# A fused attention, Fourier and feed-forward kernel: ScalarE and GpSimd in program order, weight splits two products ahead

## The chip, the core and the metric

The kernel runs on one core of a Trainium2 chip. The metric is the device time of one execution in microseconds (us), as the median of several runs. The core has five engines that run side by side: TensorE (PE in the profile, with its weight loads as PEld), VectorE (DVE), ScalarE (ACT), GpSimd (POOL) and SyncE (SP), which here issues the DMA transfers. Each engine works through its own list of instructions in the order in which the program was compiled; semaphores make one engine wait for another.

## What is computed

For each of 8 batches (8 heads, 576 tokens, head width 64): 32 packed queries attend to all keys, and all 576 queries attend to the 32 packed results. The result `x` is Fourier-transformed over tokens and over features, and a feed-forward network follows:

```
p_packed = softmax(p k^T / 8) v
x        = softmax(q p_packed^T / 8) p_packed        # 576 x 512 after joining heads
u        = x + real(fft(fft(x, tokens), features))
un       = (u - mean(u)) / sqrt(var(u) + 1e-6)
out      = u + relu(un @ w_ch1) @ w_ch2              # 512 -> 2048 -> 512
```

Products that need more than the fast matmul format's precision are done as three matmuls of split operands: `x = hi + lo`, ScalarE rounds `hi` (`wr_h`, `uh`, `fh`, ...), and VectorE or GpSimd subtracts to get `lo` (`wr_l`, `ul`, `fl`, ...).

## The kernel before

The 36 blocks of 128 token rows (four per batch, and one for each pair of batches with the rows left over, `R`) form nine tiles of four blocks, numbered 0 to 8 here. The loop at L698 runs the feed-forward network of one tile (`ffn`, L605) and, spread between its products, the attention and Fourier work of the next batch (`front`, L227).

A tile has 16 hidden slices. `up(j)` (L613) is 12 matmuls into the single bank `ph`; ScalarE then takes the relu into `hh` (L629) and VectorE makes `hl` (L630), which frees `ph`. `down(j)` (L633) is 12 matmuls into the four `acc` banks. TensorE's order is up(0), up(1), down(0), up(2), down(1), ..., up(15), down(14), down(15). Between the products stand 32 places, `step(0)` to `step(31)`: step 2j follows up(j), and step 2j+1 follows down(j-1). Each step draws one piece from the generator `front`, up to its next `yield`. The pieces of batches 2 to 7 stand in the third string of `ORDER` (L44), where `y` is a yield: `S` scores, `t` turned scores, `p` packed values, `d` their parts, `g` values spectrum, `U` queries, `e` less one, `m` less mean, `a` weights, `f` `r` `h` folded and their parts, each with a head group 0 or 1. After them come the two Fourier stages (`py`, L486, in steps 23 and 24) and twice spectrum and values (`pz`, `px`, steps 25 to 28). What is left of a batch, the rows `R`, is drawn first in the next tile (`chain`, L700): its spectra in step 0, its values in step 1, directly ahead of `S`.

Before the change the third string puts `S` in step 1, `t0 t1` in step 4, `p0 p1` in 5, `d0 d1` in 6, `g0` in 7, `g1` in 8, `U` in 9, `e0` in 10, `e1` in 11, and `m0 a0 m1 a1 f0 r0 h0 f1 r1 h1` in 12 to 21.

The order of work on an engine is set in two ways. From tile 1 on (L713) the engines in `MANUAL` (L52: PE and DVE) keep program order; ScalarE, GpSimd and SyncE are ordered at compile time by a planner, which goes by its own estimate of times. In tile 0 and ahead of it the planner orders all engines.

Weights: `wsplit` (L599) splits one 128x512 slice into `wr_h` (ScalarE) and `wr_l` (GpSimd), six buffers, so three slices. `up(j)` splits `w1[j]` just ahead of its own matmuls, and `w2[j]` behind the relu. At the end of a tile the next tile's blocks lose their mean (`less`, L579, tile `un`), are transposed between the matmuls of up(15), down(14) and down(15) (`moves`, L584, tile `untp`), and are split (`parts`, L593). `statistics` (L205) sums squares on ScalarE (`junk`), and `deviations` (L199) finishes the rows that are waiting at the next yield.

PSUM banks are given out in turn by `bank` (L93): three shared ones, `ph`, and the four `acc`. The loads of keys, values and queries share two buffers (`ld`).

Of the kernel before, what the change touches and what calls it, by code (L numbers as in the profile page):

```python
# [17 lines left out]
P = 128  # L18
S = 576
# [24 lines left out]
         "S y y y t0 t1 y p0 p1 y d0 d1 y g0 y g1 y U y e0 y e1 y m0 y a0 y m1 y a1 y f0 y r0 y h0 y f1 y "  # L44
         "r1 y h1 y y")
# [6 lines left out]
MANUAL = {mybir.EngineType.PE, mybir.EngineType.DVE}  # L52
# [26 lines left out]
def tile_kernel(ctx, tc, kpT, qT, v, w1, w2, tabC, tabS, tabR, tabB, tabT, sel, ident_d, out):  # L79
# [117 lines left out]
    late = []  # L197

    def deviations():  # L199
        while late:  # L200
            st = stat_of[late.pop(0)]
            nc.vector.tensor_scalar(st[:, 2:3], st[:, 2:3], 1.0 / DM, 1e-6, ALU.mult, ALU.add)  # L202
            nc.gpsimd.tensor_tensor(st[:, 2:3], st[:, 2:3], mhalf, ALU.pow)

    def statistics(key):  # L205
        st = stat_of[key]
        nc.vector.tensor_scalar(st[:, 1:2], st[:, 0:1], 1.0 / DM, None, ALU.mult)  # L207
        junk = work.tile([P, DM], F32, tag="tmp", name="junk", bufs=3)
        nc.scalar.activation(junk, u_of[key], AF.Square, bias=st[:, 1:2], scale=-1.0, accum_out=st[:, 2:3])  # L209
        late.append(key)  # L210
# [16 lines left out]
    def front(b):  # L227
# [3 lines left out]
        eos, fs, sums, turned = {}, {}, {}, {}  # L231
# [52 lines left out]
        def turned_scores(g):  # L284
            e1, sm2 = e1s[g], sums[g]
            ri = small.tile([P, 1], F32, tag="ri", name="ri")
            nc.vector.tensor_scalar(ri, sm2[:, 0:1], sm2[:, 1:2], 1e-9, ALU.add, ALU.add)
            nc.vector.reciprocal(ri, ri)
            rinv[g] = ri
            et = work.tile([P, 5, P], F32, tag="att", name="e1T", bufs=ATT)  # L290
            tp = bank("e1tp")
            for c in range(4):
                nc.tensor.transpose(tp[:, c * P:(c + 1) * P], e1[:, c * P:(c + 1) * P], ident)
            nc.scalar.copy(et[:, 0:4, :].rearrange("p c k -> p (c k)"), tp)
            if b < 2 or g == 0:
                turned["tq"] = bank("e1tq")
            tp = turned["tq"][:, g * P:(g + 1) * P]
            nc.tensor.transpose(tp[:D], e1[:, 4 * P:S], ident)
            nc.vector.tensor_copy(et[:D, 4, :], tp[:D])
            e1T[g] = et  # L300

        def packed(g):

            if g not in vts:
                load_values(g)
            vt = vts[g]
            po = bank("po")
            for c in range(5):
                kk = P if c < 4 else D
                for h in range(4):  # L310
                    nc.tensor.matmul(  # L311
                        po[h * NPK:(h + 1) * NPK, :D], e1T[g][:kk, c, h * NPK:(h + 1) * NPK],
                        vt[:kk, c, h * D:(h + 1) * D], start=(c == 0), stop=(c == 4),
                        tile_position=(0, h * NPK))
            pp2 = work.tile([P, 2, D], F32, tag="pp2", name="pp2")
            nc.vector.tensor_scalar(pp2, po[:, :D].unsqueeze(1).to_broadcast([P, 2, D]), rinv[g], None, ALU.mult)
            pp2s[g] = pp2

        def packed_parts(g):
# [12 lines left out]
            bd = work.tile([P, 4, D], F32, tag="tmp", name="bd", bufs=3)  # L332
            nc.gpsimd.tensor_tensor(bd, pp2[:, 0:1, :].to_broadcast([P, 4, D]),
                                    bmask.unsqueeze(2).to_broadcast([P, 4, D]), ALU.mult)
            hi = work.tile([P, 4 * D], F32R, tag="bdh", name="bdh")
            lo = work.tile([P, 4 * D], F32R, tag="bdl", name="bdl")
            split(hi, lo, bd.rearrange("p a d -> p (a d)"), nc.gpsimd)
            bdh[g], bdl[g] = hi, lo
# [19 lines left out]
        def less_one(g):  # L358

            s2 = s2s[g]  # L360
            m = small.tile([P, 18], F32, tag="m18", name="m18")
            nc.vector.tensor_reduce(m, s2, AX.X, ALU.max)  # L362
            engs[g].tensor_tensor(s2, s2, broadcast(m), ALU.subtract)  # L363
            nc.scalar.activation(s2, s2, AF.Exp, scale=0.125)
            nc.scalar.activation(s2, s2, AF.Copy, bias=-1.0)
# [12 lines left out]
        def values_spectrum(g):  # L378
# [19 lines left out]
            split(hi, lo, prod[0], TW[TL[min(b, 2)]])  # L398
            gh[g], gl[g] = hi, lo

# [22 lines left out]
        def folded_rest(g):  # L423
# [22 lines left out]
            sm.tensor_scalar(f[:, FA + 33:FA + 64], a[:, NE + 256:S], 2.0, 1.0 / 16, ALU.mult, ALU.add)  # L446

        def folded_parts(g):

            eo, f = eos[g], fs[g]  # L450
            ec, oc = eo[:, 0, :], eo[:, 1, :]
            hi = work.tile([P, FW], F32R, tag="fh", name="fh")
            lo = work.tile([P, FW], F32R, tag="fl", name="fl")
            split(hi, lo, f)
            fh[g], fl[g] = hi, lo
            hi = work.tile([P, 256], F32R, tag="xh", name="xh")
            lo = work.tile([P, 256], F32R, tag="xl", name="xl")
            nc.scalar.activation(hi, ec[:, 0:256], AF.Copy, bias=1.0 / 16)
            nc.vector.scalar_tensor_tensor(lo, ec[:, 0:256], 1.0 / 16, hi.bitcast(F32), ALU.add, ALU.subtract)
            xh[g], xl[g] = hi, lo  # L460
            hi = work.tile([P, 256], F32R, tag="oh", name="oh")
            lo = work.tile([P, 256], F32R, tag="ol", name="ol")
            split(hi, lo, oc[:, 0:256], (nc.vector, nc.gpsimd)[EO[min(b, 2)]])
            oh[g], ol[g] = hi, lo

        parts = {"S": lambda _: scores(0, 1), "U": lambda _: queries(0, 1), "s": scores, "t": turned_scores, "p": packed, "d": packed_parts, "q": queries, "e": less_one,
                 "m": less_mean, "g": values_spectrum, "a": weights, "f": folded, "r": folded_rest,
# [4 lines left out]
        for x in ORDER[min(b, 2)].split():  # L472
            if x == "y":
                yield
                deviations()
            else:
                parts[x[0]](int(x[1:] or 0))
# [57 lines left out]
        for c in range(2):  # L535
# [16 lines left out]
            deviations()  # L552
# [46 lines left out]
    def wsplit(src):  # L599
        hi = work.tile([P, DM], F32R, tag="wr", name="wr_h", bufs=6)  # L600
        lo = work.tile([P, DM], F32R, tag="wr", name="wr_l", bufs=6)
        split(hi, lo, src, nc.gpsimd)
        return hi, lo

    def ffn(first, turned, step, nxt, alone):  # L605
# [7 lines left out]
        def up(j, moves=()):  # L613
            moves = list(moves)
            wh, wl = wsplit(w1f[:, j, :])
# [5 lines left out]
            for t in (slice(i, i + step) for i in range(0, T, step)):  # L621
                for k in range(12):
                    c, (l, r) = k // 3, ((wh, uh), (wh, ul), (wl, uh))[k % 3]
                    nc.tensor.matmul(ph[:, t], l[:, c * P:(c + 1) * P], r[:, c, t], start=(k == 0), stop=(k == 11))  # L624
                    if moves:
                        moves.pop(0)()
            hh = work.tile([P, 512], F32R, tag="hh", name="hh")
# [3 lines left out]
            return (hh, hl) + wsplit(w2f[:, j, :])  # L631

        def down(j, hh, hl, vh, vl, moves=()):  # L633

            moves = list(moves)
            for i in range(n):
# [5 lines left out]

        prev = None
        for j in range(NJ):
            last = nxt is not None and j == NJ - 1
            cur = up(j, nxt.moves(0) + nxt.moves(1) if last else ())
# [6 lines left out]
            if nxt is not None and j == NJ - 2:  # L655
                nxt.less(0)
                nxt.less(1)
            if prev is not None:
                down(j - 1, *prev, [lambda: None] * 8 + nxt.moves(2) if last else ())
            step(2 * j + 1)  # L660
            if last:
                nxt.parts(2)
# [4 lines left out]
        deviations()  # L667
# [25 lines left out]
    deviations()  # L693
    spare.clear()
    rest = iter(())
    for j in range(ORDER[0].count("D"), LEAD):
        load_weights(j)
    for t, (first, tk) in enumerate(tiles):  # L698
# [118 lines left out]
```

## Time and profile before

| | us |
|---|---|
| median of 3 runs (lowest, highest) | 1069.37 (1067.02, 1071.57) |
| the profiled execution's own time | 1067.58 |
| its span, first to last instruction | 1065.8 |
| ahead of the first feed-forward product | 59.3 |
| tile 0, to the last output of it | to 200.8 |
| tiles 1 to 6, one batch's front in each | 200.8 to 884.2, 113.2 to 115.0 each |
| tile 7, with the rest of batch 7 alone | 91.9 |
| tile 8, with no front | 85.7 |

A tile's end is taken here where VectorE begins the last of the four instructions of L670 (`u` plus the network's result). Matmuls are pipelined: a 128x512 matmul is shown as 0.39 us long, and the next one starts 0.23 us behind it. So an idle time that the profile shows for PE leaves out what the modelled end covers.

### The profile page before, as it was taken

What the parts mean: (1) busy time and instruction counts of PE and PEld (TensorE: products, weight loads), DVE (VectorE), ACT (ScalarE), POOL (GpSimd) and SP (SyncE); (2) the same over time, 40 slices, a digit from 0 to 9 for tenths busy, and PEclk for the clock granted to TensorE, in tenths of its full rate; (3) what the DMA queues carried; (4) which work ended last, traced back from release to release, by engine and by line L of the source; (5) the groups of instructions that cost most, each with busy time, mean ns of one, the idle gap of its engine ahead of it and who ended that gap; (6) DMA issues with size and microseconds to landing.
All of it is one profiled execution on the core that took longest, in us unless ns stands there. A gap on an engine that the chain in (4) does not pass through costs nothing.

```text
span 1065.8 us, 15006 instructions
## 1 busy us (share of the span) xinstructions
PE 992.6 (93%) x5692; PEld 793.2 (74%) x5692; DVE 598.0 (56%) x1296; ACT 435.4 (41%) x883; POOL 471.2 (44%) x419
## 2 busy tenths in 40 slices
PE   6488888999999999999999999899999999999998
PEld 2366667767877788778877787678777888888886
DVE  4889999547553764468444846475537743113112
ACT  3544454434343444344443444344434443333332
POOL 1545644354444543455335433544445434444442
PEclk8689999999999999999999999999999999999999
DMA  8216433210012100310022002110030001001001
GB/s 328 96 45 209 131 111 101 89 65 28 2 40 95 47 2 1 115 66 1 1 90 92 1 1 83 52 47 1 31 104 1 1 2 40 1 1 40 1 1 40
DMA packets 17743, 58.65 MB, mean 55 GB/s; under 512 B 2081, under 2 KB 2465, under 8 KB 17670
## 3 DMA queue, kind: packets, MB, share of 16 engines
q1 hardware_dynamic: 17670, 57.68, 15.9%
q8 instruction: 45, 0.74, 0.3%
q14 instruction: 28, 0.23, 0.1%
HBM read 48.24 MB, written 9.44 MB: 54 GB/s over the span
## 4 chain that ended last, share of the span: by engine, by line
PE 70%; DVE 16%; ACT 7%; POOL 3%; issue 3%; DMA 1%; SPq 0%; ACTq 0%; DVEq 0%; POOLq 0%
PE ph L624 32%; PE acc L639 26%; ACT wr_h L100 2%; ACT hh L629 2%; PE untp L589 2%; POOL wr_l L101 2%; DVE turned L397 1%; DVE hl L630 1%; DVE s L363 1%; PE po L311 1%; DVE ubuf L547 1%; DVE m L362 1%; DVE turned L393 1%; PE s L255 1%; DVE w2f L181 1%
## 5 line engine op out<-in xcount | busy, mean ns | idle before, releaser
L101 POOL TENSOR_TENSOR wr_l<-w1f,wr_h 128x512 fp32r<-128x512 f32 x144 | 192.2, 1334 | 303.2 <-ACT wr_h L100 277.0
L630 DVE SCALAR_TENSOR_TENSOR hl<-ph,hh 128x512 fp32r<-128x512 f32 x144 | 99.1, 688 | 363.4 <-ACT hh L629 362.7
L101 POOL TENSOR_TENSOR wr_l<-w2f,wr_h 128x512 fp32r<-128x512 f32 x144 | 196.6, 1365 | 211.0 <-ACT wr_h L100 164.2
L624 PE MATMUL ph<-uh,wr_h 128*128 128x512 f32 (+1 forms) x580 | 232.8, 401 | 15.3 <-DVE hl L630 7.5
L624 PE MATMUL ph<-uh,wr_l 128*128 128x512 f32 (+1 forms) x580 | 230.7, 398 | 4.6 <-POOL wr_l L101 4.6
L639 PE MATMUL acc<-wr_h,hh 128*128 128x512 f32 x576 | 229.8, 399 | 4.1 <-ACT hh L629 4.1
L639 PE MATMUL acc<-wr_l,hh 128*128 128x512 f32 x576 | 228.4, 397 | 2.6 <-POOL wr_l L101 2.6
L624 PE MATMUL ph<-ul,wr_h 128*128 128x512 f32 (+1 forms) x580 | 229.4, 396 | 0.2 <-DVE ul L101 0.2
L639 PE MATMUL acc<-wr_h,hl 128*128 128x512 f32 x576 | 226.1, 393 | 0.0
L100 ACT CAST wr_h<-w1f 128x512 fp32r<-128x512 f32 x144 | 89.2, 620 | 213.2 <-PE ph L624 192.8
L100 ACT CAST wr_h<-w2f 128x512 fp32r<-128x512 f32 x144 | 89.3, 620 | 197.0 <-PE acc L639 178.0
L624 PEld LDWEIGHTS ph<-uh,wr_h 128*128 128x128 f32 x580 | 110.0, 190 | 55.0 <-DVE hl L630 13.6
L624 PEld LDWEIGHTS ph<-uh,wr_l 128*128 128x128 f32 x580 | 109.8, 189 | 33.8 <-POOL wr_l L101 10.6
L639 PEld LDWEIGHTS acc<-wr_h,hh 128*128 128x128 f32 x576 | 109.6, 190 | 27.4 <-ACT hh L629 4.8
L639 PEld LDWEIGHTS acc<-wr_l,hh 128*128 128x128 f32 x576 | 109.0, 189 | 25.3 <-POOL wr_l L101 2.9
L624 PEld LDWEIGHTS ph<-ul,wr_h 128*128 128x128 f32 x580 | 110.3, 190 | 23.1 <-DVE stat L202 0.9
L639 PEld LDWEIGHTS acc<-wr_h,hl 128*128 128x128 f32 x576 | 108.5, 188 | 23.3
L629 ACT ACTIVATE hh<-ph 128x512 fp32r<-128x512 f32 x144 | 85.2, 592 | 9.4 <-PE ph L624 9.4
L589 PE MATMUL untp<-ident,un 128*128 128x128 f32 x144 | 37.7, 278 | 5.8 <-DVE un L582 5.1
L223 PE MATMUL py<-gh,fh 128*128 128x258 f32 x64 | 18.8, 301 | 17.7 <-ACT fh L100 16.6
L209 ACT ACTIVATE junk<-ubuf,stat 128x512 f32<-128x512 f32 x36 | 25.8, 716 | 16.1 <-DVE stat L207 16.1
L101 DVE TENSOR_TENSOR ul<-untp,uh 128x512 fp32r<-128x512 f32 x36 | 23.9, 684 | 10.1 <-ACT uh L100 10.1
(205 smaller groups left out, 1306.5 us busy)
## 6 DMA issues: line engine op xcount, KB each, us to landing
kp<-kpT SPq DMA_DIRECT2D x16, 608.0 KB, 4.8
out<-ubuf SPq DMA_DIRECT2D x36, 256.0 KB, 2.1
vt<-v SPq DMA_DIRECT2D x14, 640.0 KB, 4.8
wst<-w SPq DMA_DIRECT2D x17, 512.0 KB, 3.7
qt<-qT SPq DMA_DIRECT2D x14, 576.0 KB, 4.8
ubuf<-w SPq DMA_DIRECT2D x9, 512.0 KB, 3.8
w1f<-w SPq DMA_DIRECT2D x3, 512.0 KB, 11.0
w2f<-w SPq DMA_DIRECT2D x3, 512.0 KB, 11.2
```

Of the source, the lines that this page charges most:

```text
L100: nc.scalar.copy(hi, src)
L101: (lo_eng or nc.vector).tensor_tensor(lo, src, hi.bitcast(F32), ALU.subtract)
L181: nc.vector.scalar_tensor_tensor(c, low, 29, c, ALU.logical_shift_right, ALU.bitwise_or)
L209: nc.scalar.activation(junk, u_of[key], AF.Square, bias=st[:, 1:2], scale=-1.0, accum_out=st[:, 2:3])
L223: nc.tensor.matmul(o, lh, rh, start=first, stop=False)
L255: nc.tensor.matmul(res[g][c][at, :w.stop - w.start], lhs(g, h), rhs(g, h, w), start=True, stop=True, tile_position=(r, h * NPK))
L311: nc.tensor.matmul(po[h * NPK:(h + 1) * NPK, :D], e1T[g][:kk, c, h * NPK:(h + 1) * NPK], vt[:kk, c, h * D:(h + 1) * D], start=(c == 0), st ...
L589: nc.tensor.transpose(tp[:, c * P:(c + 1) * P], un[:, c * P:(c + 1) * P], ident)
L624: nc.tensor.matmul(ph[:, t], l[:, c * P:(c + 1) * P], r[:, c, t], start=(k == 0), stop=(k == 11))
L629: nc.scalar.activation(hh[:, :T], ph[:, :T], AF.Relu)
L630: nc.vector.scalar_tensor_tensor(hl[:, :T], ph[:, :T], 0.0, hh[:, :T].bitcast(F32), ALU.max, ALU.subtract)
L639: nc.tensor.matmul(acc[i], l[:, w], r, start=(j == 0 and k == 0), stop=(j == NJ - 1 and k == 2))
```

## The change

- `MANUAL` also names Activation and Pool: ScalarE and GpSimd keep program order from tile 1 on, as PE and DVE do.
- `wsplits` is a generator over all slices of all tiles in the order of use; two slices are split ahead of the loop, and one more behind each product. `up` and `down` take theirs from the list `ready`.
- `after(n, what)` puts a piece n steps later (at the start of that step): the exponentials of `e`, the split of `g`'s result, the diagonal blocks' split (`bdh`, `bdl`; their product `bd` moves from `d` to `p`) and the squares come one step later, and the deviation two.
- `X` turns both groups' scores together: all transposes first, then the copies. `xh` and `oh` are made in `r`; in `h` VectorE makes `xl` and `ol` ahead of `fl`.
- The third string of `ORDER`: `S` stays in step 1; the rest's values move from step 1 to step 2; `X` is in step 3, `p0 p1` in 4, `d0 d1` in 5, `g0` in 6, `U` in 7, `g1` in 8, `e0` in 9, `e1` in 10, nothing in 11, and from `m0` in 12 on as before.
- `less` for blocks 0 and 1 stands ahead of step 28, and for blocks 2 and 3 between up(15)'s matmuls and its relu.

```diff
-         "S y y y t0 t1 y p0 p1 y d0 d1 y g0 y g1 y U y e0 y e1 y m0 y a0 y m1 y a1 y f0 y r0 y h0 y f1 y "
-         "r1 y h1 y y")
+         "S y X y p0 p1 y d0 d1 y g0 y U y g1 y e0 y e1 y y m0 y a0 y m1 y a1 y f0 y r0 y h0 y f1 y r1 y "
+         "h1 y y")
...
-MANUAL = {mybir.EngineType.PE, mybir.EngineType.DVE}
+MANUAL = {getattr(mybir.EngineType, n) for n in ("PE", "DVE", "Activation", "Pool")}
...
+    def after(n, what):
+
+        if steps[0] is None:
+            what()
+        else:
+            due.append((steps[0] + n, what))
...
+        after(1, squares)
+        after(2, deviation)
...
+        def turned_scores(*gs):
+            tp = {}
+            for g in gs:
+                tp[g] = bank("e1tp")
+                for c in range(4):
+                    nc.tensor.transpose(tp[g][:, c * P:(c + 1) * P], e1s[g][:, c * P:(c + 1) * P], ident)
+            tq = bank("e1tq")
+            for g in gs:
+                nc.tensor.transpose(tq[:D, g * P:(g + 1) * P], e1s[g][:, 4 * P:S], ident)
+            for g in gs:
+                e1T[g] = work.tile([P, 5, P], F32, tag="att", name="e1T", bufs=ATT)
+                nc.scalar.copy(e1T[g][:, 0:4, :].rearrange("p c k -> p (c k)"), tp[g])
+                nc.vector.tensor_copy(e1T[g][:D, 4, :], tq[:D, g * P:(g + 1) * P])
...
+            after(1, diagonals)
...
-            nc.scalar.activation(s2, s2, AF.Exp, scale=0.125)
-            nc.scalar.activation(s2, s2, AF.Copy, bias=-1.0)
+
+            def exps():
+                nc.scalar.activation(s2, s2, AF.Exp, scale=0.125)
+                nc.scalar.activation(s2, s2, AF.Copy, bias=-1.0)
+
+            after(1, exps)
...
-            split(hi, lo, prod[0], TW[TL[min(b, 2)]])
             gh[g], gl[g] = hi, lo
+            after(1, lambda: split(hi, lo, prod[0], TW[TL[min(b, 2)]]))
...
+    def wsplits():
+
+        for _ in tiles:
+            for n, j in [(0, 0)] + [x for j in range(1, NJ) for x in ((0, j), (1, j - 1))] + [(1, NJ - 1)]:
+                hi = work.tile([P, DM], F32R, tag="wr", name="wr_h", bufs=6)
+                lo = work.tile([P, DM], F32R, tag="wr", name="wr_l", bufs=6)
+                split(hi, lo, (w1f, w2f)[n][:, j, :], nc.gpsimd)
+                ready.append((hi, lo))
+                yield
...
             if last:
-                nxt.less(2)
-                nxt.less(3)
+                cur = up(j, nxt.moves(0) + nxt.moves(1), lambda: less(2, 3))
                 nxt.parts(0)
                 nxt.parts(1)
+            else:
+                cur = up(j)
+            next(splits, None)
+            if nxt is not None and j == NJ - 2:
+                less(0, 1)
             step(2 * j)
...
-        gen = chain(rest, front(t + 1) if t + 1 < B else iter(()))
+        gen = front(t + 1) if t + 1 < B else iter(())
...
-            if not ended and next(gen, None) == "rest":
+            next_step()
+            if t > 0 and i in (0, 2):
+                next(rest, None)
+            elif not ended and next(gen, None) == "rest":
                 ended.append(gen)
```

More of the change, by code (lines that the diff above doesn't have):

```diff
@@ L1 @@
 from contextlib import ExitStack, nullcontext
-from itertools import chain
 import numpy as np
@@ L196, in tile_kernel, with next_step, statistics, squares @@
     now = {}
[L197 to L201, printed above, removed]
+    due = []
+    steps = [None]
+    def after(n, what):
[3 more added lines that the diff above has]
+            due.append((steps[0] + n, what))
+    def next_step():
+        steps[0] = (steps[0] or 0) + 1
+        for item in [x for x in due if x[0] <= steps[0]]:
+            due.remove(item)
+            item[1]()
+    def statistics(key):
+        st, u = stat_of[key], u_of[key]
+        nc.vector.tensor_scalar(st[:, 1:2], st[:, 0:1], 1.0 / DM, None, ALU.mult)
+        def squares():
+            junk = work.tile([P, DM], F32, tag="tmp", name="junk", bufs=3)
+            nc.scalar.activation(junk, u, AF.Square, bias=st[:, 1:2], scale=-1.0, accum_out=st[:, 2:3])
+        def deviation():
             nc.vector.tensor_scalar(st[:, 2:3], st[:, 2:3], 1.0 / DM, 1e-6, ALU.mult, ALU.add)
             nc.gpsimd.tensor_tensor(st[:, 2:3], st[:, 2:3], mhalf, ALU.pow)
[L205 to L210, printed above, removed]
+        after(1, squares)
+        after(2, deviation)
     def load(src, shape, name, place=None):
@@ L282, in scores @@
                 e1s[g], sums[g] = e1, sm2
[L284 to L300, printed above, removed]
+        def turned_scores(*gs):
[11 more added lines that the diff above has]
+                nc.vector.tensor_copy(e1T[g][:D, 4, :], tq[:D, g * P:(g + 1) * P])
+            for g in gs:
+                ri, sm2 = small.tile([P, 1], F32, tag="ri", name="ri"), sums[g]
+                nc.vector.tensor_scalar(ri, sm2[:, 0:1], sm2[:, 1:2], 1e-9, ALU.add, ALU.add)
+                nc.vector.reciprocal(ri, ri)
+                rinv[g] = ri
         def packed(g):
@@ L446, in folded_rest @@
             sm.tensor_scalar(f[:, FA + 33:FA + 64], a[:, NE + 256:S], 2.0, 1.0 / 16, ALU.mult, ALU.add)
+            xh[g] = work.tile([P, 256], F32R, tag="xh", name="xh")
+            nc.scalar.activation(xh[g], ec[:, 0:256], AF.Copy, bias=1.0 / 16)
+            oh[g] = work.tile([P, 256], F32R, tag="oh", name="oh")
+            nc.scalar.copy(oh[g], oc[:, 0:256])
         def folded_parts(g):
@@ L451, in folded_parts @@
             ec, oc = eo[:, 0, :], eo[:, 1, :]
[L452 to L467, printed above, removed]
+            fh[g] = work.tile([P, FW], F32R, tag="fh", name="fh")
+            nc.scalar.copy(fh[g], f)
+            xl[g] = work.tile([P, 256], F32R, tag="xl", name="xl")
+            nc.vector.scalar_tensor_tensor(xl[g], ec[:, 0:256], 1.0 / 16, xh[g].bitcast(F32), ALU.add, ALU.subtract)
+            ol[g] = work.tile([P, 256], F32R, tag="ol", name="ol")
+            (nc.vector, nc.gpsimd)[EO[min(b, 2)]].tensor_tensor(ol[g], oc[:, 0:256], oh[g].bitcast(F32), ALU.subtract)
+            fl[g] = work.tile([P, FW], F32R, tag="fl", name="fl")
+            nc.vector.tensor_tensor(fl[g], f, fh[g].bitcast(F32), ALU.subtract)
+        parts = {"S": lambda _: scores(0, 1), "U": lambda _: queries(0, 1), "X": lambda _: turned_scores(0, 1),
+                 "s": scores, "t": turned_scores, "p": packed, "d": packed_parts, "q": queries, "e": less_one, "m": less_mean, "g": values_spectrum, "a": weights, "f": folded, "r": folded_rest,
                  "h": folded_parts,
@@ L611, in ffn, with up @@
         now["acc"] = acc
-        def up(j, moves=()):
+        def up(j, moves=(), between=lambda: None):
             moves = list(moves)
-            wh, wl = wsplit(w1f[:, j, :])
+            wh, wl = ready.pop(0)
             pool, tag = (ps, "ps") if alone and j % 2 else (psf, "ph")
@@ L641, in down, with less @@
                         moves.pop(0)()
+        def less(*ks):
+            for k in ks:
+                nxt.less(k)
         prev = None
@@ L666, in ffn @@
             nxt.parts(3)
-        deviations()
+        next(splits, None)
         for i, key in enumerate(keys):
```

42 lines of the change are left out of this document (18 added, 24 removed).

## The prediction

> **What bounds the kernel.** The page's first lines come first: which engine is busy.
>
> ```profile
> PE 992.6 (93%) x5692; PEld 793.2 (74%) x5692; DVE 598.0 (56%) x1296; ACT 435.4 (41%) x883; POOL 471.2 (44%) x419
> ```
>
> TensorE is busy for 993 of 1066 us, so no change of order can win more than its idle time. The busy time by stretches says where that lies (columns: length, then busy time and instructions of each engine, granted clock, DMA).
>
> ```profile
> 0.00:60.00 60.00, 32.65 (x266) 21.70 (x267) 41.04 (x97) 27.18 (x61) 19.91 (x47) 0.78 0.53 189
> 60.00:200.80 140.80, 121.76 (x668) 94.11 (x668) 126.96 (x242) 64.47 (x127) 68.80 (x55) 0.95 0.37 115
> 200.80:884.20 683.40, 660.78 (x3965) 531.20 (x3964) 395.11 (x905) 286.51 (x594) 301.64 (x256) 1.00 0.12 41
> 884.20:976.10 91.90, 91.76 (x421) 75.57 (x420) 20.25 (x35) 31.18 (x56) 42.43 (x34) 1.00 0.03 12
> 976.10:1061.80 85.70, 85.63 (x378) 70.59 (x376) 13.83 (x21) 26.05 (x45) 38.40 (x30) 1.00 0.04 13
> ```
>
> The reader is to see three kernels in one. Up to 200.8 us (the opening and tile 0) PE loses 46 us, and in tile 0 VectorE, which decodes the weights, is busy for 127 of 141 us: it is the bound there. In tiles 1 to 6 PE loses 22.6 us of 683.4. Tiles 7 and 8 lose 0.2 us together and have nothing to give. The change binds ScalarE and GpSimd from tile 1 on, so the 22.6 us come first: what does PE wait for there?
>
> ```profile
> PE e1tq L298 <- DVE e1T L299: 7.6, 6, 1.3
> PE ph L624 <- DVE s L356: 6.5, 6, 1.1
> PE untp L589 <- DVE un L582: 3.5, 8, 0.5
> PE ph L624 <- POOL wr_l L101: 3.3, 9, 0.4
> PE ph L624 <- DVE stat L202: 1.2, 3, 0.4
> ```
>
> This is the whole list of waits for that stretch (total, times, longest): 22.1 us in 32 waits, the same few places in each tile. Each costs more than it shows, since the next matmul could have started before the modelled end of the last:
>
> ```profile
> 316.22 0.39 PE L624 MATMUL ph<-uh,wr_h 128*128 128x512 f32 x1
> 316.45 0.39 PE L624 MATMUL ph<-ul,wr_h 128*128 128x512 f32 x1
> ```
>
> Starts are 0.23 us apart and lengths 0.39, so a wait hides another 0.16: 32 x 0.16 = 5.1. The five places hold 22.1 + 5.1 = **27.2 us**.
>
> **Part by part.** *The paired transposes.* PE waits before `e1tq` of group 1, because VectorE still copies group 0 out of the same bank. In `X` both `e1tq` transposes come before the first copy, and the three tiles take the three banks in turn. The wait goes: 7.6 + 6 x 0.16 = 8.6. What could be late next is the exponentials:
>
> ```profile
> 324.00 0.21 ACT L280 ACTIVATION_READ_ACCUMULATOR e<-s,nb 128x1 f32 x1
> 326.08 0.39 PE L624 MATMUL ph<-uh,wr_h 128*128 128x512 f32 x1
> ```
>
> In tile 2 the last ended at 324.2, and `X` now stands where up(2) began, at 326. With the values of `R` moved behind up(1), VectorE's maxima for `S` start earlier still. I cost the new waits at 0.
>
> *The queries, `U`.* It takes `ph`, and up(4) must wait until VectorE has turned `ph`'s tail. VectorE is late because of `g1`, one step ahead:
>
> ```profile
> 342.98 1.29 DVE L393 TENSOR_TENSOR turned<-pg,turn 128x516 f32<-128x516 f32 x2
> 345.25 0.29 PE L387 MATMUL pg<-basis,pph 128*128 128x258 f32 x1
> 348.74 1.24 PE L255 MATMUL s2T<-qt,ppT 64*32 64x512 f32 x16
> 348.88 1.89 DVE L397 TENSOR_TENSOR turned<-turned 128x258 f32<-128x258 f32 x2
> 350.69 0.37 DVE L356 STREAM_TRANSPOSE s<-s2Tt 128x64 f32<-128x64 f32 x2
> ```
>
> Afterwards `g0` is one step ahead instead, the same VectorE work. What changes is its start: `hl` waits for a relu that the planner put behind a weight split and `gh`. In program order the relu comes first and `gh` a step later. Counted from the end of the up ahead: 0.65 (relu) + 0.69 (`hl`) + 1.3 (two products, L393) + 1.9 (two sums, L397, at their slowest) = 4.5, and the tail is turned at 4.8; on PE the queries follow `pg`'s start, which is that end, by 348.74 - 345.25 = 3.5, and end 1.0 later at 4.5. A wait of 0.3 to 0.4 stays, 2.1 us over six tiles, of 6.5 + 1.0 = 7.5.
>
> *Splits two ahead, exponentials a step later.* The chain of waits shows what held up(7) of tile 2:
>
> ```profile
> 359.24 0.69 ACT s L364
> 359.96 0.69 ACT s L365
> 360.64 0.49 ACT hh L629
> 361.13 0.52 ACT wr_h L100
> 361.72 1.30 POOL wr_l L101
> 363.06 2.57 PE ph L624 x10
> 365.63 2.72 PE acc L639 x12
> ```
>
> The exponentials stand ahead of the relu, and the split that up(7) needs is behind both. Now `e0` and `e1` are a step earlier, their exponentials (two of 0.69 a group) in steps 10 and 11, both done before up(6) ends, and the split is one product older. The 3.3 us of `wr_l` go with their 1.4 hidden. No new slack is endless: the split for up(j+1) now stands behind relu j, and is ready 0.03 + 0.51 + 0.62 + 0.08 + 1.31 = 2.55 after up(j) ends; its weight load is due at 2.72 (down(j-1)) + 0.45 - 0.19 = 2.98. That leaves 0.4, more where front work stands between. Buffers cost nothing: a new split overwrites the product before the last.
>
> *The means ahead of step 28, and ahead of the relu.* `un` waits behind the products of step 28; moved ahead, all of it is ready when up(15) begins. 3.5 + 8 x 0.16 = 4.8 goes. `hl(14)` stays ahead; pe and qe come 1.3 later, which nothing on PE awaits. The 1.2 us on the statistics of `R` go too (1.7 with the hidden part), since up(2) no longer stands behind them.
>
> *Hidden pieces.* Twice a tile an up starts late without a listed wait:
>
> ```profile
> 379.18 0.19 PEld L624 LDWEIGHTS ph<-uh,wr_h 128*128 128x128 f32 x1 [0.37 <-DVE hl L630]
> ```
>
> `ph` is freed late as the relu stood behind `fh` and a split. Two matmuls then start 0.11 late each: 0.22 x 2 x 6 = 2.6 us, which go with the relu put first.
>
> *What the relu first costs.* This is the part to distrust. In the planner's order the split runs ahead of the relu:
>
> ```profile
> 353.92 0.62 ACT L100 CAST wr_h<-w1f 128x512 fp32r<-128x512 f32 x1 [2.50 <-PE ph L624]
> 354.45 0.59 ACT L629 ACTIVATE hh<-ph 128x512 fp32r<-128x512 f32 x1
> 354.62 1.31 POOL L101 TENSOR_TENSOR wr_l<-w1f,wr_h 128x512 fp32r<-128x512 f32 x1 [1.80 <-ACT wr_h L100]
> 355.07 0.69 DVE L630 SCALAR_TENSOR_TENSOR hl<-ph,hh 128x512 fp32r<-128x512 f32 x1 [2.82 <-ACT hh L629]
> ```
>
> GpSimd's subtraction lies over VectorE's wait and over `hl`, which reads PSUM. With the relu first it starts 0.5 later, when `hl` is nearly over, and two of them follow each other, beside the front's operations on VectorE. Those do not go well together:
>
> ```profile
> L459 DVE SCALAR_TENSOR_TENSOR xl<-eo,xh x16: 409/1526/1533, 35.9 to 843.9; 128x256 fp32r<-128x256 f32 x16
> 362.05:390.45 28.40, 28.05 (x122) 22.33 (x121) 24.44 (x60) 11.53 (x22) 14.96 (x11) 1.00 0.00 1
> ```
>
> One operation takes 0.41 us alone and 1.53 beside `wr_l`. In the ten products from 362 to 390 us, where `m` to `h` run, VectorE is busy 24.4 of 28.4 us already (third engine of the row). The Trainium skill (SBUF — State Buffer, section "Who interferes with whom") says that a VectorE instruction with two SBUF inputs and a GpSimd instruction that reads SBUF exclude each other for the whole instruction; 0.41 + 1.12, nearly a whole subtraction, agrees. By that rule alone each of the eleven subtractions there could hold VectorE up in full; without it the order would cost nothing. The cost lies between 0 (no stall of PE) and 11 x 1.12 = 12.3 us of VectorE a tile less what is lost there already. I walk through the tightest place, `f0` and `r0` behind up(8):
>
> ```profile
> 372.69 0.57 DVE L415 TENSOR_TENSOR eo<-a 128x287 f32<-128x287 f32 x1
> 374.36 0.54 DVE L433 TENSOR_TENSOR f<-eo 128x45 f32<-128x45 f32 x4
> ```
>
> `f0` takes 374.36 - 372.69 = 1.7, and `r0` some 1.5. From up(8)'s end `hl` runs to 1.6 (`a1` is late), the first operation of `f0` waits for `wr_l` to 2.5 and runs to 3.0, the second waits for the next to 4.3, and `f0` ends at 5.6. `r0` is caught by the third subtraction at 5.4 + 1.2 = 6.7 and ends at 8.4; `hl(9)` ends at 9.0, where up(10) wanted `ph` at 5.4 + 2.7 = 8.1. I take this 0.9 once a tile, 5.4 us.
>
> *The rest.* DMA: SyncE stays with the planner.
>
> ```profile
> 320.68 0.81 SPq L219 DMA_DIRECT2D vt<-v  x2
> vt<-v SPq DMA_DIRECT2D x14, 640.0 KB, 4.8
> ```
>
> Values load once `S` has read the keys, 320.7 in tile 2, and land 4.8 later; `p` is behind two ups, a down and `X`, some 9 us later. Queries load behind `p`, and three products lie between it and `U`, 8 us: 0. GpSimd's `bd`, `bdl`, `gl` and the powers fit into 5.4 - 2.6 us a pair of products: 0. Opening and tile 0: the planner still orders them, VectorE has the same work, and PE's longest waits there are for the relu and `hl`, behind that work. I take 0, and for the ends +8 (each of 16 slices loses half of a 1.12 us overlap more, 9) and -8:
>
> ```profile
> PE ph L624 <- DVE hl L630: 7.5, 4, 2.4
> PE acc L639 <- ACT hh L629: 4.1, 2, 3.3
> ```
>
> **The sum.** Removed: 27.2 + 2.6 = 29.8. Kept or added: 2.1 + 5.4 = 7.5. The gain is 22.3, and 1067.6 (the profiled execution; its span of 1065.8 leaves 1.8 around it) less 22.3 is **1045 us**. The median of the runs shown, 1069.4, is 1.8 above that execution; I leave the forecast at 1045 and let the range cover it.
>
> **The rivals.** *VectorE becomes the bound in steps 12 to 22* (0.20). For it: 24.4 busy of 28.4, and the order above. If the time lost to subtractions there grows by half of the 12.3 (6.1 us), VectorE needs 30.5 us, where PE wants 27.2 (ten times 2.72); 3.3 a tile instead of 0.9 is 14 us more: 1059. Against it: reductions and `hl` do not collide, and steps 9 to 11 leave VectorE time. It is what the rule cited above from the Trainium skill would do at its hardest.
>
> *Tile 0 takes back what the others gain* (0.08). VectorE has 14 us free there, in 141; splits a product earlier put ScalarE's relus behind weights that are not decoded. One us in each of 16 slices and the 9 above is 25 us: about 1070, no change. Against it: the planner sees readiness, if only estimated.
>
> *The low parts come late on every up* (0.09, the other side). If a VectorE operation holds the port as `wr_l` starts, the 2.55 above grows by up to `fl`'s 1.0, and PE stalls for whatever exceeds 2.98. A stall of 0.6 in 15 ups of 6 tiles is 54 us: 1045 + 54 = 1099. It decides from 0.25 us per up (22.3 / 90). Against it: VectorE is in `hl` when `wr_l` starts, at least after most ups.
>
> *The order of ScalarE and GpSimd does nothing* (0.03): the planner's order were program order. The rows at 353.92 speak against it. `X` and the means alone would give 8.6 + 4.8: 1054.
>
> **How the numbers follow.** My forecast, with gains of 15 to 35 us, has 0.60. Measurements of this kernel tell about 0.5% (5.3 us) from no change. Faster: 0.60 + 0.20 + 0.03 = 0.83; same 0.08; slower 0.09. The range runs from 1033 (nothing kept or added, and some of the -8 of tile 0) to 1062 (the VectorE rival and its spread): it leaves out the last two real rivals and a little on both sides.
>
> **What would show it.** After the change the list of PE's waits in tiles 1 to 6 should lack `e1tq` on `e1T`, `untp` on `un` and `ph` on `wr_l`, and keep a shorter `ph` on `s` (L356). Tiles 1 to 6 should be 108.5 to 111 us long and lose the 1 us between odd and even tiles; tiles 7 and 8 stay. ScalarE should wait for PE in front of the relu, not of `wr_h`. VectorE's L403, L397 and `xl` should have longer means if the port counts, and `ph` should wait for `hl` in step 17. I am wrong if the gain lies ahead of 200.8 us, if `wr_l` heads the waits, or if tiles 1 to 6 stay over 112.

## The result, and the profile after

| | before | after |
|---|---|---|
| median, us (lowest, highest; 4 runs each) | 1069.81 (1067.02, 1071.57) | 1039.76 (1037.38, 1041.16) |
| the profiled execution, us | 1067.58 | 1041.16 |
| tiles 1 to 6, us | 683.3 | 654.2 |
| tiles 7 and 8, us | 92.0, 85.7 | 91.9, 85.8 |

The ratio is 0.9719 (95% interval 0.9689 to 0.9749): 30 us faster. Where did the time go? First the busy time by stretches of the changed kernel, cut at its own tile ends (columns as in the prediction):

```profile
0.00:60.00 60.00, 32.19 (x263) 21.92 (x264) 39.83 (x94) 26.94 (x60) 19.98 (x47) 0.86 0.53 189
60.00:203.70 143.70, 123.16 (x672) 94.79 (x672) 128.53 (x246) 63.38 (x128) 68.91 (x54) 0.93 0.37 113
203.70:857.80 654.10, 649.00 (x3964) 534.09 (x3963) 428.72 (x904) 280.80 (x594) 300.24 (x255) 1.00 0.12 43
857.80:949.70 91.90, 91.90 (x422) 75.74 (x421) 23.91 (x35) 29.61 (x56) 42.20 (x33) 1.00 0.03 12
```

Only the third row has changed: tiles 1 to 6 lost 29 us. Tile 0 ends 2.9 us later in this execution; over those kernels below that leave tile 0 as it is in the changed one, that end lies anywhere from 199.7 to 204.8, so this is spread. PE's idle time in tiles 1 to 6 is 5.1 us instead of 22.6. VectorE's busy time has risen from 395 to 429 us with the same work (905 and 904 instructions). All of PE's waits in that stretch (who waits, for whom; total, times, longest):

```profile
PE acc L665 <- POOL wr_l L100: 3.1, 6, 0.5
PE ph L648 <- DVE s L375: 2.0, 6, 0.3
```

Four of the five old places are gone and the fifth is down from 6.5 us to 2.0, as forecast. The first row is a new wait, once a tile, in down(15). The timeline of tile 2 shows what it stands behind (start, length, engine, line; last the wait and its releaser):

```profile
413.38 0.71 ACT L218 ACTIVATE junk<-ubuf,stat 128x512 f32<-128x512 f32 x1
...
414.09 0.58 ACT L654 ACTIVATE hh<-ph 128x512 fp32r<-128x512 f32 x1
414.57 1.06 ACT L99 CAST uh<-untp 128x512 fp32r<-128x512 f32 x2
...
415.51 0.64 ACT L99 CAST wr_h<-w2f 128x512 fp32r<-128x512 f32 x1
416.23 1.30 POOL L100 TENSOR_TENSOR wr_l<-w2f,wr_h 128x512 fp32r<-128x512 f32 x1 [4.89 <-ACT wr_h L99]
...
417.58 0.50 PE L665 MATMUL acc<-wr_l,hh 128*128 128x512 f32 x1 [0.54 <-POOL wr_l L100]
```

In program order the last split of the tile is behind the relu and two `uh`; its low part ends at 417.53, and the second matmul of down(15) waits 0.54 for it. The relu is late itself: up(15) ends at 413.50 by the profile, and two sums of squares (`junk`) hold ScalarE until the relu begins, 0.59 later.

### The profile page after: what moved, and what is told of

The parts are those of the page before. It is cut to its first block, busy times and chain, and to the rows that moved or that the text cites. A ratio compares the mean times of both kernels' runs of the same rounds, so it can differ in the third digit from the quotient of the medians.

```text
span 1039.4 us, 14908 instructions
## 1 busy us (share of the span) xinstructions
PE 981.9 (94%) x5692; PEld 797.1 (77%) x5692; DVE 635.6 (61%) x1296; ACT 425.7 (41%) x883; POOL 470.1 (45%) x419
## 4 chain that ended last, share of the span: by engine, by line
PE 74%; DVE 16%; ACT 4%; issue 3%; DMA 2%; POOL 2%; SPq 0%; ACTq 0%; DVEq 0%; POOLq 0%
PE ph L648 33%; PE acc L665 30%; DVE ubuf L568 2%; DVE turned L420 1%; PE po L327 1%; DVE w1f L181 1%; DVE w2f L180 1%; DVE hl L655 1%; DMA wst<-w 1%; ACT hh L654 1%; DVE turned L416 1%; ACT junk L218 1%; DVE w2f L181 1%; PE s L270 1%; DVE w1f L180 1%
## 5 line engine op out<-in xcount | busy, mean ns | idle before, releaser
L100 POOL TENSOR_TENSOR gl<-turned,gh 128x516 fp32r<-128x516 f32 x16 | 24.5, 1532 | 23.4 <-ACT gh L99 22.4
```

What stands on the lines that cost most here:

```text
L100: (lo_eng or nc.vector).tensor_tensor(lo, src, hi.bitcast(F32), ALU.subtract)
```

## The experiments

Of the 27.7 us of waits that the forecast takes away, it gives 12.7 to the new order of ScalarE and GpSimd with the splits ahead of it: 5.4 at the queries, 4.7 at `wr_l` and 2.6 in hidden pieces. The rival is that the moves of single pieces carry all of it. Twelve kernels took the change apart; each ran once unless noted, beside runs of the kernel before with medians of 1066.9 to 1069.3 us.

### The order alone, and the change without it

*Before, with all four engines in program order:*

```diff
-MANUAL = {mybir.EngineType.PE, mybir.EngineType.DVE}
+MANUAL = {getattr(mybir.EngineType, n) for n in ("PE", "DVE", "Activation", "Pool")}
```

> The kernel before, with program order for ScalarE and GpSimd from tile 1 on and nothing else of the change. Theory (program order pays only with splits ahead): the split for up(j) is written into buffers that down(j-2) frees right before up(j), so each up waits for 0.6 + 1.3 us less what its first matmuls cover, 1.5 to 2 us in some 120 ups: tiles 1 to 8 grow by 22 to 30 us each, the kernel to 1250 to 1310. Rival (program order by itself is the gain): at most 1060, tiles 1 to 6 at most 112.

1369.22 us, slower by 300: the kind was as expected, the size beyond it. Program order alone does great harm.

*The changed kernel, with the planner for ScalarE and GpSimd again:*

```diff
-MANUAL = {getattr(mybir.EngineType, n) for n in ("PE", "DVE", "Activation", "Pool")}
+MANUAL = {getattr(mybir.EngineType, n) for n in ("PE", "DVE")}
```

> The changed kernel, but ScalarE and GpSimd are ordered by the planner again; all else of the change stays. Theory (program order serves the relu and the splits): the transposes' and the means' gains stay, while the waits on wr_l and the late hl come back, 3.3 + 1.4 + 2.6 us or about 7 in tiles 1 to 6, so these are some 110.2 us long instead of 109.0 and the kernel takes about 1047. Rival (the pieces' places make the gain, and the planner does as well with them): tiles 1 to 6 within 0.3 us of 109.0, the kernel within 2 us of the changed one.

1034.50 us, tiles 1 to 6 in 650.1 and no wait of PE left in them. My theory expected a loss and fell: with the rest of the change in place, program order is not what gained. So the parts were taken away one by one, under both orders.

### Pieces not put later, splits not ahead

`after` at once, in the steps of the loop:

```diff
-        if steps[0] is None:
+        if steps[0] is None or steps[0] > 2 * NJ:
             what()
```

> The changed kernel, but from tile 1 on the exponentials, the split of g, the diagonal blocks' split, the squares and the deviations are put in their own step again, not one or two later. Theory (in program order a ScalarE piece in the same step as the VectorE work it needs holds the next relu): the relus behind e0, e1, g0 and g1 start 0.5 to 2 us late, and with hl behind them ph is late in some of four ups a tile: 1 to 3 us a tile, 6 to 18 in all, 1046 to 1058. Rival (splits two ahead alone give enough slack): within 2 us of the changed kernel.

> The kernel with ScalarE and GpSimd left to the planner and the rest of the change, but from tile 1 on the exponentials, splits of g, diagonal blocks, squares and deviations stand in their own step again. Tiles 1 to 6 took 650.1 us together with them later. Theory (the planner finds room for such pieces by itself, since it moves them behind work that is ready): 650 to 654. Rival (being later is what makes them fit, in either order): 660 to 676, as program order without them showed 676.1.

The condition holds for every step of tiles 1 to 8. And the splits where they were, `w1` at the start of its up, `w2` behind the relu:

```diff
...
-            wh, wl = ready.pop(0)
+            wh, wl = one_split(w1f[:, j, :])
...
-            return hh, hl
-
-        def down(j, hh, hl, moves=()):
+            return hh, hl, one_split(w2f[:, j, :])
+
+        def down(j, hh, hl, weights, moves=()):
...
```

> The kernel with ScalarE and GpSimd left to the planner and the rest of the change, but each weight slice is split where it was before, w1's ahead of its up and w2's behind the relu, in all tiles. Theory (with the planner the splits two ahead take away the waits on wr_l, 3.3 + 1.4 us in tiles 1 to 6, and part of the late relus, 2.6): tiles 1 to 6 take 655 to 658 together instead of 650.1. Rival (the planner already reaches far enough ahead): 650 to 652. Second rival (splits two ahead are most of the gain): over 665.

> The changed kernel, all four engines in program order, pieces a step later, but the weight splits issued where they were before (w1 at the start of its up, w2 right behind the relu). Theory: in program order the split two ahead is needed, since ScalarE takes the split for up(j) only behind the front pieces of the step ahead, and these wait for PE and VectorE; some 1 to 1.5 us at each of the ten products that have pieces, tiles 1 to 6 together 700 to 760 us (after: 654.2), time 1085 to 1145, PE's waits there headed by wr_h and wr_l. Rival: the pieces put later are enough, and the splits ahead add as little in program order as they add with the planner (650.0 against 650.1): 650 to 660 us, time 1035 to 1046.

> Of the change only the moves of pieces: the planner orders ScalarE and GpSimd as before, splits stand where they stood before, exponentials, squares, values' split and diagonals are not put later; new are X, the order string of the front, the means ahead of step 28 and of the relu, the rest's values a step later, and the two copies moved from h to r. Theory (the moves carry the gain, program order, splits ahead and later pieces add nothing together): tiles 1 to 6 in 650 to 656 us (before 683.3, after 654.2), time 1034 to 1041, none of the five waits of before left but a small one on s or hl. Rival (the forecast's: the splits ahead and the relu put first carry 4.7 + 1.4 + 2.6 and part of the 7.5 on s): the waits on wr_l stay and the odd and even tiles differ by 1 us; 662 to 668 us, time 1047 to 1053.

| the changed kernel with | planner: time, tiles 1 to 6 | program order: time, tiles 1 to 6 |
|---|---|---|
| splits ahead and pieces later | 1034.50, 650.1 | 1039.76, 654.2 (the change) |
| splits ahead only | 1036.61, 654.0 | 1060.49, 676.1 |
| pieces later only | 1034.6, 650.0 | 1379.97, 957.3 |
| neither, the moves alone | 1039.18, 653.4 | not run |

Read the left column first. The moves alone (`X`, the order string, the means earlier, the rest's values a step later, two copies from `h` to `r`) bring 30 us, as much as the whole change. (That kernel also has smaller parts of the change, among them `bd` in `p`, `parts(2)` ahead of step 31, and the deviations, which stand right behind their squares instead of at the next yield.) With the planner the splits ahead add nothing (650.0 against 650.1), and the later pieces some 3 to 4 us of tiles 1 to 6. Here is that moves-only kernel; its list of PE's waits is empty, although its splits stand where they stood before:

```profile
202.90:856.30 653.40, 652.88 (x3964) 532.19 (x3963) 381.88 (x904) 288.91 (x594) 304.84 (x256) 1.00 0.12 43
```

The opposite kernel, with program order, splits ahead and later pieces but the old places in the string, was not run. So the moves are shown to be enough with the planner; how much the other parts would win without them stays open.

The right column says what program order needs. Without the later pieces tiles 1 to 6 lose 22 us, more than the 6 to 18 that I expected, and at another place. Not `ph` is late but the weights of two downs in each tile:

```profile
PE acc L665 <- POOL wr_l L100: 13.8, 12, 1.2
PE acc L665 <- ACT wr_h L99: 3.6, 6, 0.6
```

In tile 2 one split stands behind `gl` on GpSimd, and at the tile's end the split for down(14) stands behind squares that wait for VectorE. Without the splits ahead the six tiles lose 303 us, PE's waits being

```profile
PE ph L654 <- ACT wr_h L99: 131.4, 71, 4.0
PE ph L654 <- POOL wr_l L100: 64.9, 83, 1.9
```

I had expected 700 to 760 us for those six tiles, and pieces of the front as the cause; 957.3 came out, and tile 8, which has no front, went from 85.8 to 104.3 as well. Its timeline (the same kernel) has the reason; `w1f` is the source of the next up's split:

```profile
1311.25 0.60 ACT L660 ACTIVATE hh<-ph 128x512 fp32r<-128x512 f32 x1 [4.76 <-PE ph L654]
1311.75 0.61 ACT L99 CAST wr_h<-w2f 128x512 fp32r<-128x512 f32 x1
1312.26 0.62 ACT L99 CAST wr_h<-w1f 128x512 fp32r<-128x512 f32 x1
1312.43 1.31 POOL L100 TENSOR_TENSOR wr_l<-w2f,wr_h 128x512 fp32r<-128x512 f32 x1 [3.84 <-ACT wr_h L99]
1313.71 1.28 POOL L100 TENSOR_TENSOR wr_l<-w1f,wr_h 128x512 fp32r<-128x512 f32 x1
1315.04 0.50 PE L654 MATMUL ph<-uh,wr_l 128*128 128x512 f32 x1 [0.65 <-POOL wr_l L100]
```

The split for the next up is third in line, behind the relu and the split of `w2`; two subtractions on GpSimd follow each other, and the low part is ready at 1314.99, 3.7 us after the relu begins, where a down lasts 2.7. So even without a front each up is late. The planner puts that split ahead of the relu and needs no list of splits for it, as tile 8 of the moves-only kernel shows:

```profile
973.36 0.62 ACT L99 CAST wr_h<-w1f 128x512 fp32r<-128x512 f32 x1 [2.15 <-PE ph L654]
973.89 0.59 ACT L660 ACTIVATE hh<-ph 128x512 fp32r<-128x512 f32 x1
```

### Single moves undone, in the changed kernel

*Scores turned in turn, as before:* `X` calls the old order of copies for each group, with one `e1tq` bank for both.

```diff
...
+                tq = bank("e1tq") if tq is None else tq
+                nc.tensor.transpose(tq[:D, g * P:(g + 1) * P], e1s[g][:, 4 * P:S], ident)
+                nc.vector.tensor_copy(e1T[g][:D, 4, :], tq[:D, g * P:(g + 1) * P])
...
```

> The changed kernel, but from batch 2 on step 3 turns the two groups' scores in turn as before, the second e1tq behind VectorE's copy of the first from the same bank. Theory: PE waits there again for 1.28 us seen and 0.16 hidden in each of tiles 1 to 6, 8.6 us in all: about 1048, tiles 110.4. Rival (PE would only wait later for the copies, in p): within 2 us of the changed kernel.

1044.98 us, tiles 1 to 6 in 661.0: 6.8 more (8.6 expected), with the old wait back.

```profile
PE e1tq L312 <- DVE e1T L313: 5.8, 6, 1.5
```

*The means late, as before:* `less(2, 3)` behind the relu, `less(0, 1)` behind step 28, from tile 1 on.

```diff
-                cur = up(j, nxt.moves(0) + nxt.moves(1), lambda: less(2, 3))
+                cur = up(j, nxt.moves(0) + nxt.moves(1), (lambda: None) if first else (lambda: less(2, 3)))
+                if first:
+                    less(2, 3)
...
-            if nxt is not None and j == NJ - 2:
+            if nxt is not None and j == NJ - 2 and not first:
                 less(0, 1)
             step(2 * j)
+            if nxt is not None and j == NJ - 2 and first:
+                less(0, 1)
```

> The changed kernel (program order), but from tile 1 on the means are taken off behind step 28 and behind the relu of up(15), as before. Theory: PE waits for un again, 3.5 us seen and 1.3 hidden: tiles 1 to 6 take 659 together instead of 654.2. Rival (with ScalarE in program order the relu comes sooner and un is ready anyway): 654 to 655.

1045.67 us, tiles 1 to 6 in 659.2: 5.0 more, and the wait is the old one.

```profile
PE untp L609 <- DVE un L602: 7.0, 6, 1.2
```

The 659 that I expected came out by luck. The wait is longer than the 3.5 us of before, and the wait of down(15) for `wr_l`, 3.1 us in the changed kernel, is gone from the list: the 5.0 is the net of the two.

### The two waits that were left

*The split of up(15) ahead of `parts(0)` and `parts(1)`*, from tile 1 on:

```diff
+                if first:
+                    next(splits, None)
                 nxt.parts(0)
                 nxt.parts(1)
             else:
                 cur = up(j)
-            next(splits, None)
+            if not (last and first):
+                next(splits, None)
```

> The changed kernel (program order), but from tile 1 on the split behind up(15) stands ahead of the parts of blocks 0 and 1 on ScalarE and GpSimd, not behind them. Theory (the new wait of down(15) on wr_l, 3.1 us seen and 1.0 hidden, is the price of that place in the queue): the wait is gone, tiles 1 to 6 take 650 together instead of 654.2. Rival (GpSimd's two powers hold that wr_l): 653 to 654.

1034.56 us, tiles 1 to 6 in 649.3, and only `ph` for `s` is left. That one place is worth 4.9 us, more than all that program order lost against the planner (654.2 against 650.1).

*In addition `U` two steps later*, behind `g1`, which comes one step earlier; `e0` and `e1` come one later and take the step that was empty:

```diff
-         "S y X y p0 p1 y d0 d1 y g0 y U y g1 y e0 y e1 y y m0 y a0 y m1 y a1 y f0 y r0 y h0 y f1 y r1 y "
+         "S y X y p0 p1 y d0 d1 y g0 y g1 y y U y e0 y e1 y m0 y a0 y m1 y a1 y f0 y r0 y h0 y f1 y r1 y "
```

> The changed kernel in program order, with the split in up(15) put ahead of parts 0 and 1 from tile 1 on (as in e7) and U put two steps later, behind g1, in step 9. Theory: the wait of acc for wr_l stays gone (649.3 us in e7), and the tail of the queries is turned while no product of g is ahead of it on VectorE, so the 1.9 us of ph for s and its 6 x 0.16 hidden go too: tiles 1 to 6 in 646.5 to 648 us, time 1031 to 1034. Rival: the split of gl or e0 right behind makes it late again, or e0 waits for its queries: 649 to 653 us, time 1034 to 1040.

This is the fastest version found: 1032.84 us median of 5 runs (1031.41 to 1034.63), ratio to before 0.9665 (0.9651 to 0.9678), below the interval of the change. The single runs of 1034.5 to 1034.6 above lie within its range; what sets it apart from them is tiles 1 to 6, in 647.1 instead of 649.3 to 650.1. PE is busy there without a gap that the profile shows:

```profile
202.20:849.30 647.10, 647.10 (x3964) 534.15 (x3963) 429.66 (x904) 279.97 (x594) 301.37 (x255) 1.00 0.13 43
```

### VectorE's slack

*Three more reductions in each `r`*, whose results nothing uses:

```diff
+            if b >= 2:
+                for _ in range(3):
+                    pad = small.tile([P, 18], F32, tag="pad", name="pad")
+                    nc.vector.tensor_reduce(pad, a.rearrange("p (a k) -> p a k", a=18), AX.X, ALU.max)
```

> The changed kernel with three more reductions of 128x576 on VectorE (0.74 us each by the rows of the same size) at the end of each r from the front of tile 2 on: 4.4 us of VectorE a tile. Theory: VectorE had some 1.3 us of slack at hl(9) in the changed kernel (hl ends at 372.0, up(10) wants ph at about 373.3), so 2.2 us a group exceed it by 0.9: 0.9 to 1.8 us a tile, tiles 1 to 6 in 659 to 665 us, with ph waiting for hl as PE's new first wait. Rival 1, VectorE bounds steps 12 to 22 (the forecast's): all of it shows, 4.4 a tile, 680 us. Rival 2, it has far more room: 654 to 656 us.

```profile
L473 DVE TENSOR_REDUCE pad<-a 128x18 f32<-128x576 f32 x36 | 24.7, 737 | 0.0
...
PE py L240 <- DVE fl L490: 6.4, 4, 1.6
PE ph L652 <- DVE hl L659: 3.8, 6, 0.6
```

1055.07 us, tiles 1 to 6 in 666.9: of 24.7 us of added work 12.7 show, less than if VectorE were the bound (all of it), and more than the 5 to 11 that I expected, since `fl` at the end of `h1` is late too, once in each of tiles 2 to 5. So VectorE had about 2 us a tile to spare in steps 12 to 22 (4.1 added, 2.1 shown), and it is the next bound there.

## Why the prediction was right, and where it was not

The time (1045 forecast, 1039.76 measured) and the place (tiles 1 to 6) were right. That the sum came so near is in part luck: it hides errors in both directions, and one wrong cause.

The ledger of tiles 1 to 6: for each matmul, the distance from the start of the one ahead less the median distance behind a matmul of that kind (by the tile that it writes), added up by the tile that the late matmul writes. This counts also what a modelled end hides. The forecast's terms stand beside it:

| gain in us | forecast | measured |
|---|---|---|
| `e1tq` | 8.6 | 8.4 |
| `untp` (the means) | 4.8 | 6.3 |
| `ph` (forecast: on `s` 5.4, `wr_l` 4.7, `stat` 1.7, hidden 2.6) | 14.4 | 17.8 |
| `s2T` (the queries' products) | 0 | 1.1 |
| relu first, VectorE held up | -5.4 | 0 |
| `acc` in down(15) | 0 | -4.8 |
| sum | 22.4 | 28.7 |

- **Paired transposes, means:** right, the means a little too small; undone singly they cost 6.8 and 5.0, where the 5.0 has the vanished wait of down(15) in it (by the ledger 7.7 more at `untp` and 2.9 less at `acc`).
- **Queries:** 2.1 were to stay, and 2.0 stayed; putting `U` behind `g1` removed them (649.3 to 647.1). The size was exact; that program order is what wins the rest fell with the moves-only kernel, which has no such wait.
- **Hidden pieces:** mis-sized. I took 0.16 us behind each listed wait, 5.1 in all, and 2.6 in unlisted ones. By the same ledger the excess of before is 47.9 us, against 12.2 in the fastest version, so 35.7 were there to be won, not 29.8. 22.1 of it are listed. Some 4.7 more lie on the very matmuls that waited, 0.15 each, as I had it. The other 8.9, where I had 2.6, lie on matmuls that follow them and at places without a listed wait. So the bound that the prediction begins with, PE's idle time, is too low: 22.6 us were idle in tiles 1 to 6, and the fastest version is 36.2 shorter there, since PE's busy time by its modelled ends fell too, from 660.8 to 647.1.
- **What the relu first costs:** the step that failed. The collision with GpSimd came as described, but the stall did not:

```profile
366.43 1.31 POOL L100 TENSOR_TENSOR wr_l<-w1f,wr_h 128x512 fp32r<-128x512 f32 x1 [2.85 <-ACT wr_h L99]
367.70 1.53 POOL L100 TENSOR_TENSOR wr_l<-w2f,wr_h 128x512 fp32r<-128x512 f32 x1
366.63 1.43 DVE L438 TENSOR_TENSOR eo<-a 128x287 f32<-128x287 f32 x1
367.98 1.56 DVE L439 TENSOR_TENSOR eo<-a 128x287 f32<-128x287 f32 x1
...
371.32 0.69 DVE L655 SCALAR_TENSOR_TENSOR hl<-ph,hh 128x512 fp32r<-128x512 f32 x1
```

Each of the first two operations of `f0` took about 1.5 us instead of 0.5 (rows of tile 2 of the changed kernel; GpSimd's first), ending with the subtraction beside it. Yet `hl(9)` ended at 372.0, and up(10) took `ph` at 373.2: `r0` took 1.0 and not the 1.5 that I put in, no third subtraction caught it, and `hl(8)` was done at 366.7, early. So the 5.4 us had no stall behind them: PE's list has no wait for `hl`. I had counted VectorE's lost time as if it had no slack. The Trainium skill (SBUF — State Buffer, "Who interferes with whom") states that a VectorE instruction with two SBUF inputs contends with a GpSimd instruction that reads SBUF, and these rows agree. But where the collision falls decides what it costs. The same sums of `g` in three kernels, before, changed, and changed with the planner (busy time, mean ns of one):

```profile
L397 DVE TENSOR_TENSOR turned<-turned 128x258 f32<-128x258 f32 x24 | 15.9, 705 | 0.4
```

```profile
L420 DVE TENSOR_TENSOR turned<-turned 128x258 f32<-128x258 f32 x24 | 21.9, 951 | 0.4
```

```profile
L420 DVE TENSOR_TENSOR turned<-turned 128x258 f32<-128x258 f32 x24 | 9.2, 424 | 0.4
```

PE noticed none of it: VectorE is busy for 430 us in the fastest version and for 381 in the planner's, with the same 904 instructions. Of the three operations that were to become longer only these sums did (L397, 0.71 to 0.95). `xl` became shorter (1.53 to 0.97), while `ol` beside it grew (0.41 to 0.97), and the weights' product at L403 became shorter too (1.25 to 0.76).

- **Missed:** the wait in down(15), 3.1 us listed and 4.9 when it was removed. I had counted the slack of a split behind one relu (0.4 us), and wrote "more where front work stands between" without walking through the end of a tile, where two `uh` (1.06 together) stand between and the squares hold the relu.
- **Splits ahead, program order:** the wait for `wr_l` went, but it did not need the reason given, since it goes with the moves alone; whether that reason would have been enough without the moves was not run. What the forecast called one step is a pair that cancels: program order makes the splits ahead necessary, and these make it harmless. The rival "the order does nothing" (0.03) was right that the order wins nothing, but not in its reason, that the planner's order were program order: alone, program order costs 300 us. Its 1054 is too high, as I credited it with `X` and the means only; the moves-only kernel shows that the other moves take the waits on `s`, `wr_l` and `stat` with them. Which of these moves takes which was not separated. The step without a piece behind `e1` is not needed for it, at least beside the splits ahead: the fastest version has `m0` right behind it and PE has no wait.
- **The other rivals:** VectorE was not the bound, but 2 us a tile from it. Tile 0 took nothing back beyond its spread. Low parts late on most ups is what the two slow kernels do (83 waits for `wr_l` in the 96 ups of tiles 1 to 6 in the slower one); with the splits two ahead they are late once a tile.

## What to carry to other kernels

Take a change that has several parts apart in both directions before crediting one of them: here program order, which names the change, costs 4 us beside the other parts, and the moves bring 30 without it. An engine in program order needs its work issued as early as a planner would have hoisted it; walk through the last slice of a tile as well as the steady ones. Busy time that grows on an engine with slack is no loss. What the profile lists as PE's waits is not all that can be won: here 22.1 us were listed, and 36.2 were won.

## What was unexpected

Behind short pauses TensorE ran at a lower clock. In the kernel in program order without splits ahead, the mean granted clock of tiles 1 to 6 is 0.91, where it was 1.00 before and in the changed kernel. A pause in tile 2 shows it (below the matmuls, three stretches in the columns of the tables above; the granted clock is third from the end):

```profile
421.86 0.50 PE L654 MATMUL ph<-uh,wr_h 128*128 128x512 f32 x1 [2.40 <-ACT wr_h L99]
...
423.25 0.79 PE L654 MATMUL ph<-uh,wr_l 128*128 128x512 f32 x1 [0.65 <-POOL wr_l L100]
```

```profile
419.00:423.00 4.00, 1.20 (x5) 0.34 (x3) 0.87 (x1) 2.05 (x4) 1.37 (x2) 0.95 0.00 0
423.00:427.00 4.00, 3.75 (x9) 2.98 (x10) 0.00 (x0) 0.00 (x0) 0.20 (x1) 0.50 0.00 0
427.00:431.00 4.00, 4.00 (x14) 3.13 (x13) 2.38 (x4) 1.62 (x3) 1.90 (x2) 0.70 0.00 0
```

If the clock was either full or half, these means make it half for some 0.4, 4.0 and 2.4 us, 6.8 in all, beginning near 422.6: behind the pause of 2.40 us and two matmuls, with the wait of 0.65 already in it. The Trainium skill (TensorE: Matmul & The Clock Gate, "What's actually happening") puts the drop behind an idle window of about 3.4 us; here the pause was 2.40. The kernel in program order without the later pieces shows the same at the end of tile 2, where PE's pauses are 0.6 and 1.2 us:

```profile
416.20:419.60 3.40, 3.40 (x10) 2.52 (x9) 0.38 (x1) 0.00 (x0) 1.30 (x1) 0.50 0.02 5
```

Whether the share of idle time in a stretch decides it was not tested. Of the 310 us that the tiles 1 to 6 of the kernel without splits ahead have above the fastest version's, PE's listed waits are 196. The other 114 are longer busy time of PE (761 us instead of 647), much of it, by estimate, matmuls at the lower clock.
